# Moving four quotients and a reciprocal around the output projections of an attention and MLP kernel

## The chip, the cores and the metric

The kernel runs on one core of one Trainium2 chip. The metric is device time in microseconds (us) of the whole program. Three timed runs of the kernel before gave a median of 3466.72 us (3463.46 to 3468.94). One more execution was recorded by the profiler; all times of single instructions below come from that one.

The engines are named as the profile names them: PE multiplies matrices (PEld loads its weights), DVE, ACT and POOL work on vectors, SP issues most of the DMA transfers. Each engine takes its instructions in the order in which the program has them, and an instruction that waits holds back all behind it.

## The reference

Two layers, each of attention and an MLP, on one sequence of 2048 rows of width 512 with 32 heads of width 16, all in float32:

```python
x = x + A(layernorm(x), wqkv, wo)
x = x + B(layernorm(x), w1, b1, w2)
# and both once more with the same weights

A: p = softmax(q @ k.T * 16**-0.5);  return (p @ v) @ wo
B: h = x @ w1 + b1;  return (h * tanh(softplus(h))) @ w2        # F = 1792
```

## The kernel before

Every large product is done as three products of rounded parts: each operand is split in a high part and a low part (what is left after rounding), and high*high, high*low and low*high are summed in one PSUM bank. So an output projection tile is 12 matmuls of 128x512: 4 slices of the contraction times 3.

The rows stand in four chunks of 512 (0 to 3). Attention runs over groups of four heads and over chunks; a chunk's sum over keys (softmax not yet divided) is written to DRAM as `raw`, its softmax denominators as `rawsum`. The chunks of the last group end one after the other, and each must then be divided before it can be projected with `wo`. That is what `heads` does for a chunk, as a generator in three kinds of steps:

- first step (`behind(c)`): load the denominators into `sums`, and `raw` into the buffer `ol`.
- second step (`invert(c)`): the reciprocal of `sums` on DVE (line 576); store it to a DRAM scratch `inv` (line 578); load it back, spread over the 16 rows of each head, by eight transfers of 128 KB into the buffer `oh` (line 581). All of these transfers are issued by SP.
- then four steps (`divide(c)`), one for each slice k of the contraction: the quotient `on` = `ol` * `oh` (on DVE for even k, line 590; on POOL for odd k, line 588), its high part cast into `oh` (line 591) and the low part into `ol` (line 592), both on DVE. Each quotient needs all eight transfers.

`project(c)` then does the four tiles t of a chunk: 12 matmuls into a bank of PSUM, then one DVE add of the bank to the residual `x2` (line 607). There are two such banks (tag "n"), so the matmuls of tile t+2 wait for the add of tile t. After each tile's add a function is called that puts other work at this place: `stats` in chunk 0, `middle` in chunk 1, `late` in chunk 2. They advance `norm_steps` (the layer norm of chunk 0 for the MLP: four statistics steps, then steps that scale a tile into `xnm`, transpose it on PE into `tpm`, and split it into `thm` and `tlm`), and they advance the division of the chunks 2 and 3. Chunks 0 and 1 are divided while attention still runs.

The order around the change is written out by hand: `Order` ties each instruction of an engine to the one recorded before it, for the PE, DVE and some ACT instructions of this part. Everything else (the statistics of the later chunks, the MLP's first matmuls `h`, the DMAs) is set between them by a scheduler that goes by the place in the program. SP's transfers all go to one hardware queue, in the order of the code: `load_w1` brings parts 2 to 6 of the first MLP weight (1 MB each; parts 0 and 1 are loaded earlier), `load_w2` those of the second.

Of the kernel before, what the change touches and what calls it, by code (L numbers as in the profile page):

```python
# [51 lines left out]
def kernel(ctx: ExitStack, tc: tile.TileContext, x, wqkv, wo, w1, b1, w2, out):  # L52
# [21 lines left out]
    def b8(shape, dt, name):  # L74
        return blk.tile(shape, dt, tag="blk", name=name)
# [3 lines left out]
    def pbank(tag, name):  # L79
        return ps.tile([P, 512], F32, tag=tag, name=name, bufs=PS_BUFS[tag])  # L80
# [63 lines left out]
    def fetch(kind, j, name):  # L144
        _, a, b = view(kind, j)
        t = b8([P, 2, a, b], F32R, name)
        nc.sync.dma_start(t.bitcast(F32), wparts[kind, j])
        return t
# [12 lines left out]
    def mm3(acc, pairs, first=True, last=True, pe=lambda ins: ins):  # L161
        n = len(pairs)
        for i, (ah, al, bh, bl) in enumerate(pairs):
            pe(nc.tensor.matmul(acc, ah, bh, start=first and i == 0, stop=False))  # L164
            pe(nc.tensor.matmul(acc, ah, bl, start=False, stop=False))  # L165
            pe(nc.tensor.matmul(acc, al, bh, start=False, stop=last and i == n - 1))  # L166

    def norm_parts(src, nm, got, key, tag, fine=False, o=lambda ins: ins):
# [21 lines left out]
        if fine:  # L190
            stats(0)
            rstd(0, 1)
# [18 lines left out]
    def spread(hooks, at, src, nm, got, key):  # L211
        parts = norm_parts(src, nm, got, key, "acc")
        for c, f in at:
            hooks.setdefault((c, f), []).append(lambda: next(parts, None))
# [244 lines left out]
    def load_qkv(l, wts, which, **kw):  # L459
        for j in which:  # L460
            kind, i = ("qk", j) if j < 4 else ("v", j - 4)
            wts[j] = make(kind, i, hi="act", **kw) if l == 0 else fetch(kind, i, f"{kind}{l}{i}")
# [103 lines left out]
    def heads(att, c, o=free):  # L566
        l = att.l
        w = H * CW // P
        sums = t512("he", f"sums{l}{c}")[:, 0:w]
        nc.sync.dma_start(sums, att.sums[c].rearrange("h (x j) -> (h x) j", j=w))  # L570
        ol = b8([P, KT, CW], F32R, f"ol{l}{c}")
        oh = b8([P, KT, CW], F32R, f"oh{l}{c}")
        x, r = ol.bitcast(F32), oh.bitcast(F32)
        nc.sync.dma_start(x, att.raw[c].rearrange("(k p) q -> p k q", p=P))
        yield
        o(nc.vector.reciprocal(sums, sums))
        inv = dram.tile([H, CW], F32, name=f"inv{l}{c}")
        nc.sync.dma_start(inv.rearrange("h (x j) -> (h x) j", j=w), sums)
        n = P // DH
        for h in range(n):  # L580
            nc.sync.dma_start(
                r[ts(h, DH)], inv[h::n, :].unsqueeze(0).to_broadcast([DH, KT, CW])
            )
        yield (oh, ol)
        for k in range(KT):
            on = t512("f", f"on{l}{c}{k}")
            if k % 2:
                nc.gpsimd.tensor_tensor(on, x[:, k], r[:, k], op=ALU.mult)
            else:
                o(nc.vector.tensor_tensor(on, x[:, k], r[:, k], op=ALU.mult))  # L590
            o(nc.vector.tensor_copy(oh[:, k], on))
            o(nc.vector.tensor_tensor(ol[:, k], on, r[:, k], op=ALU.subtract))
            yield

    def project(l, c, parts, wot, x2, o=free, behind=None):
        oh, ol = parts
        for t in range(NCH):
            acc = pbank("n", f"wo{l}{c}{t}")
            mm3(
                acc,  # L600
                [
                    (oh[:, k, ts(t, P)], ol[:, k, ts(t, P)], wot[k // 2][:, 0, k % 2], wot[k // 2][:, 1, k % 2])
                    for k in range(KT)
                ],
                pe=o,
            )
            o(nc.vector.tensor_tensor(x2[:, t], acc, x2[:, t], op=ALU.add))
            if behind:
                behind(t)
# [195 lines left out]
    for l in range(2):  # L805
        if l == 0:
            order = [(m, 0) for m in (0, 4, 1, 5, 2, 6)] + [(m, 1) for m in (0, 4, 1, 5)] + [(3, 0)]
            order += [(0, 2), (4, 2), (7, 0), (2, 1), (6, 1), (0, 3), (4, 3)]
        else:
            order = [(0, 0), (0, 1), (0, 2), (4, 0), (4, 1), (4, 2)]  # L810
            order += [(1, 0), (5, 0), (1, 1), (5, 1), (1, 2), (0, 3), (4, 3)]
        order += [(m, c) for m in (1, 5) for c in range(NCH) if (m, c) not in order]
        order += [("v", c) for c in range(NCH)]
        order += [(m, c) for m in (2, 6, 3, 7) for c in range(NCH) if (m, c) not in order]
        att = qkv(l, wts, tt, order, before, *((front, vst0) if l == 0 else ()))
        wot, w1t, w2t, x2s, tts = [], [], [], [], {}
        xsrc = x if l == 0 else xs

        def load_res(c):
            x2 = b8([P, NCH, D], F32, f"x2{l}{c}")  # L820
            nc.sync.dma_start(x2, xsrc[ts(c, CW), :].rearrange("(t p) d -> p t d", p=P))
            x2s.append(x2)

        hooks, parts, work = {}, {}, {}

        def behind(c, o=free):
            work[c] = heads(att, c, o)
            next(work[c])

        def invert(c):  # L830
            parts[c] = next(work[c])

        def divide(c):
            next(work[c], None)

        def load_wo(i):
            wot.append(fetch("wo", i, f"wo{l}{i}"))

        def load_w1(i):
            w1t.append(fetch("w1", i, f"w1{l}{i}"))  # L840

        def load_w2(i):
            w2t.append(fetch("w2", i, f"w2{l}{i}"))

        if l == 0:
            todo = [("wo", i) for i in range(2)] + [("w1", i) for i in range(7)] + [("w2", i) for i in range(7)]
            for n, (kind, i) in enumerate(todo):
                hooks[30 + 24 * n] = lambda kind=kind, i=i: make(kind, i)
        for i in range(2):
            hooks[STEPS - GSTEPS + 2 * i + 1] = lambda i=i: load_wo(i)  # L850
            hooks[STEPS - GSTEPS + 2 * i + 5] = lambda i=i: load_res(i)
            hooks[STEPS - 1 + i] = lambda i=i: load_w1(i)
        for c, load, inv, div in ((0, 30, 22, 20), (1, 28, 21, 15), (2, 10, 7, None)):
            hooks[STEPS - load] = lambda c=c: behind(c, att.order)
            hooks[STEPS - inv] = lambda c=c: invert(c)
            for k in range(KT if div else 0):
                hooks[STEPS - div + k] = lambda c=c: divide(c)
        att.run(hooks)
        o = att.order
        behind(3, o)  # L860
        for i in range(2, 4):
            load_res(i)
        first = norm_steps(x2s[0], f"m{l}0", tts, 0, "s", o)

        def stats(t):
            next(first)
            if t >= 2:
                divide(2)
            if t == 3:
                invert(3)  # L870

        project(l, 0, parts[0], wot, x2s[0], o, stats)
        for i in range(2, 7):
            load_w1(i)
        def middle(t):
            next(first)
            if t < 2:
                divide(2)

        project(l, 1, parts[1], wot, x2s[1], o, middle)  # L880
        for i in range(4):
            load_w2(i)
        def late(t):
            if t < 2:
                next(first)
            divide(3)

        project(l, 2, parts[2], wot, x2s[2], o, late)
        project(l, 3, parts[3], wot, x2s[3], o)
        for i in range(4, 7):  # L890
            load_w2(i)
        hooks = {}
        for c in range(NCH - 1):
            spread(hooks, [(c, f) for f in range(5, 10)], x2s[c + 1], f"m{l}{c + 1}", tts, c + 1)
        wts, tt = {}, {}
        if l == 0:
            last = NCH - 1
            for f, js in ((2, (0,)), (4, (2,)), (9, (1,)), (11, (3,)), (12, (4,)), (13, (5,))):
                hooks.setdefault((last, f), []).append(lambda js=js: load_qkv(1, wts, js))
            for c in range(last):  # L900
                spread(hooks, [(last, f) for f in range(1 + 4 * c, 6 + 4 * c)], x2s[c], f"q1{c}", tt, c)
        mlp(l, x2s, w1t, w2t, tts, xs if l == 0 else out, hooks)
        if l == 0:
            before = {}
            steps(before, range(2, 12), norm_steps(x2s[last], f"q1{last}", tts, "q", "n", free))
            before.setdefault(11, []).append(lambda: tt.update({last: tts["q"]}))
# [28 lines left out]
```

## Time and profile before

| | |
|---|---|
| median of 3 runs | 3466.72 us (3463.46 to 3468.94) |
| the profiled execution: its own time | 3467.81 us |
| its span (first to last instruction) | 3466.0 us |
| mean granted clock of PE | 0.997 |
| busy: PE, DVE, ACT, POOL | 99%, 86%, 76%, 8% of the span |

A row of a timeline has the start, the duration, the engine, the line of the kernel, the operation, out<-in, the shapes and the number of merged instructions; the square bracket at its end has the idle time of the engine just before and what ended it. SPq is SP's issuing of transfers: the duration is that of issuing, not of the transfer. A row of a windows table has the stretch, its length, each engine's busy time with its instruction count, the granted clock of PE, the busy share of the DMA engines and what they moved in GB/s.

The output projections of layer 0 lie at about 1376 to 1432 us of the span, those of layer 1 at about 3103 to 3159 us.

### The profile page before, as it was taken

The numbers are of one execution on the slowest core, as the hardware profiler recorded it, in microseconds if no ns is written. First come the engines' busy times: TensorE is split into PE (matmuls) and PEld (weight loads), VectorE is DVE, ScalarE is ACT, GpSimd is POOL, SyncE is SP. The second block draws the span as 40 slices with busy tenths as digits, with TensorE's granted clock in tenths as the row PEclk, the third lists the DMA queues.
The fourth block names the chain that finished last, engine by engine and source line by source line (L and its number), as shares of the span: only waits on it lengthen the run. The fifth ranks groups of instructions, "written<-read, shape, count | busy, mean of one in ns | idle before, by whom it ended". The sixth has DMA issues, their size and how long they took to land.

```text
span 3466.0 us, 71144 instructions
## 1 busy us (share of the span) xinstructions
PE 3443.8 (99%) x29075; PEld 1917.8 (55%) x29075; DVE 2966.5 (86%) x4155; ACT 2620.2 (76%) x4865; POOL 282.1 (8%) x329
## 2 busy tenths in 40 slices
PE   9999999999999999999999999999999999999999
PEld 6644444444444445888876444444444444458887
DVE  5699999999999996665537999999999999966554
ACT  3189899989889888356522888988998999874665
POOL 1000000000000001222200000000000000012222
PEclk9999999999999999999999999999999999999999
DMA  7641312213121114500264202112020221154000
GB/s 253 233 102 35 81 43 74 61 54 81 45 58 50 37 55 109 195 13 13 86 199 156 53 15 46 26 36 43 18 56 15 46 37 25 55 136 167 13 13 25
DMA packets 131864, 247.39 MB, mean 71 GB/s; under 512 B 30929, under 2 KB 72401, under 8 KB 116433
## 3 DMA queue, kind: packets, MB, share of 16 engines
q1 hardware_dynamic: 77680, 169.43, 19.6%
q10 hardware_dynamic: 53856, 73.41, 5.8%
q8 instruction: 229, 3.75, 0.5%
q14 instruction: 99, 0.80, 0.1%
HBM read 149.43 MB, written 92.27 MB: 70 GB/s over the span
## 4 chain that ended last, share of the span: by engine, by line
PE 95%; DMA 2%; DVE 2%; ACT 1%; SPq 0%; issue 0%; DVEq 0%; ACTq 0%
PE pv L402 32%; PE sp L355 25%; PE pm L275 8%; PE pn L275 4%; PE h L165 3%; PE h L166 3%; PE h L164 3%; PE mo L164 3%; PE mo L165 3%; PE mo L166 3%; PE qk L164 1%; PE qk L165 1%; PE qk L166 1%; PE va L164 1%; PE va L166 1%; PE va L165 1%
## 5 line engine op out<-in xcount | busy, mean ns | idle before, releaser
L357 ACT ACTIVATE p<-sp 128x512 f32<-128x512 f32 x4040 | 2108.7, 599 | 240.9 <-PE pn L275 145.6
L308 DVE TENSOR_REDUCE mxv<-pn 128x1 f32<-128x512 f32 x2048 | 1306.2, 677 | 6.2 <-PE pn L275 4.4
L293 DVE TENSOR_REDUCE mxv<-pm 128x2 f32<-128x1024 f32 x1024 | 1241.8, 1213 | 78.6 <-PE pm L275 78.6
L355 PE MATMUL sp<-qs,ks 50*128 50x512 f32 x4040 | 1265.9, 445 | 0.0
L402 PE MATMUL pv<-p,va 128*32 128x256 f32 x16384 | 1211.7, 388 | 1.1 <-DVE pt L152 1.1
L355 PEld LDWEIGHTS sp<-qs,ks 50*128 50x128 f32 x4040 | 562.8, 184 | 689.2 <-ACT p L357 620.2
L275 PE MATMUL pn<-ks,qs 48*128 48x512 f32 x2048 | 824.8, 450 | 1.2 <-DVE mxv L308 0.9
L402 PEld LDWEIGHTS pv<-p,va 128*32 128x32 f32 x16384 | 385.0, 108 | 558.1 <-issue 428.4
L275 PE MATMUL pm<-ks,qs 48*128 48x512 f32 x2048 | 437.6, 423 | 1.4 <-DMA ks<-scr 1.4
L275 PEld LDWEIGHTS pn<-ks,qs 48*128 48x128 f32 x2048 | 366.2, 183 | 8.3 <-DVE mxv L308 2.7
L275 PEld LDWEIGHTS pm<-ks,qs 48*128 48x128 f32 x2048 | 193.5, 185 | 64.4 <-issue 7.8
L320 POOL CAST nh<-nm 128x16 fp32r<-128x16 f32 x64 | 12.6, 197 | 2436.7 <-DVE nm L315 2436.7
L666 POOL TENSOR_TENSOR hb<-hb,he 128x512 f32<-128x512 f32 x112 | 148.3, 1324 | 471.9 <-DVE he L663 471.9
L164 PE MATMUL mo<-w,ah 128*128 128x512 f32 x448 | 175.5, 392 | 3.2 <-ACT ah L669 3.0
L166 PE MATMUL h<-thm,w 128*128 128x512 f32 x448 | 175.0, 391 | 0.0
L165 PE MATMUL h<-tlm,w 128*128 128x512 f32 x448 | 174.9, 390 | 0.0
L165 PE MATMUL mo<-w,ah 128*128 128x512 f32 x448 | 174.9, 390 | 0.0
L164 PE MATMUL h<-thm,w 128*128 128x512 f32 x448 | 174.7, 391 | 0.0
L166 PE MATMUL mo<-w,al 128*128 128x512 f32 x448 | 166.1, 390 | 0.0
L668 DVE TENSOR_TENSOR hb<-hb,hr 128x512 f32<-128x512 f32 x112 | 77.3, 690 | 98.9 <-ACT hr L665 73.2
L151 ACT ACTIVATE pt<-qk 128x512 fp32r<-128x512 f32 x64 | 37.9, 598 | 147.7 <-PE qk L166 122.1
L660 ACT ACTIVATE hb<-h,b1t 128x512 f32<-128x512 f32 x112 | 76.9, 686 | 95.4 <-PE h L166 54.1
(133 smaller groups left out, 2590.2 us busy)
## 6 DMA issues: line engine op xcount, KB each, us to landing
scr<-pt ACTq DMA_DIRECT2D x64, 512.0 KB
ks<-scr SPq DMA_DIRECT2D x168, 128.0 KB
qs<-scr SPq DMA_DIRECT2D x168, 128.0 KB
vscr<-vst ACTq DMA_DIRECT2D x32, 512.0 KB
va<-vscr SPq DMA_DIRECT2D x16, 1024.0 KB
w<-w1p SPq DMA_DIRECT2D x14, 1024.0 KB
w<-w2p SPq DMA_DIRECT2D x14, 1024.0 KB
raw<-ot SPq DMA_DIRECT2D x256, 32.0 KB
```

What stands on the lines that cost most here:

```text
L164: pe(nc.tensor.matmul(acc, ah, bh, start=first and i == 0, stop=False))
L165: pe(nc.tensor.matmul(acc, ah, bl, start=False, stop=False))
L166: pe(nc.tensor.matmul(acc, al, bh, start=False, stop=last and i == n - 1))
L275: nc.tensor.matmul(out, qs[h // 2][rows, q0 : q0 + P], ks[h // 2][rows, ts(c, 512)], start=True, stop=True)
L293: self.order(nc.vector.tensor_reduce(self.mxs[b][:, 0:2, qt, c], pm, axis=AX.X, op=ALU.max))
L308: self.order(nc.vector.tensor_reduce(self.mxs[b][:, h, qt, c : c + 1], pm, axis=AX.X, op=ALU.max))
L355: nc.tensor.matmul(sp, ks[h // 2][rows, ts(kt, P)], qs[h // 2][rows, ts(qb, CW)], start=True, stop=True)
L357: return lambda: self.order(nc.scalar.activation(self.pts[s][:, h], sp, AF.Exp, scale=SCALE))
L402: nc.tensor.matmul(acc[ts(h, VW), cols], va[:, kt, h, :], self.pts[s][:, h, cols], start=kt == 0 and half == 0, stop=kt == NKT - 1, skip_g ...
L660: nc.scalar.activation(hb, acc, AF.Identity, bias=b1t[:, f : f + 1])
L666: nc.gpsimd.tensor_tensor(hb, hb, e, op=ALU.mult)
L668: nc.vector.tensor_tensor(hb, hb, r, op=ALU.mult)
```

## The change

Three edits, the same in both layers since the code is shared:

1. The first two `divide(2)` steps (slices 0 and 1 of chunk 2) stand ahead of `project` of chunk 0; before, they stood behind its tiles 2 and 3.
2. The last two `divide(2)` steps (slices 2 and 3) stand behind tiles 1 and 2 of chunk 0; before, behind tiles 0 and 1 of chunk 1.
3. `invert(3)`, chunk 3's reciprocal with its nine transfers, stands in `middle`, behind tile 0 of chunk 1 and the first scaling of the norm; before, it stood behind tile 3 of chunk 0.

```diff
         def stats(t):
             next(first)
-            if t >= 2:
+            if t in (1, 2):
                 divide(2)
-            if t == 3:
-                invert(3)
-
+
+        divide(2)
+        divide(2)
         project(l, 0, parts[0], wot, x2s[0], o, stats)
         for i in range(2, 7):
             load_w1(i)
         def middle(t):
             next(first)
-            if t < 2:
-                divide(2)
+            if t == 0:
+                invert(3)
 
         project(l, 1, parts[1], wot, x2s[1], o, middle)
```

No instruction is added or taken away. SP's queue at this place in layer 0, before (in the names, the digits behind `inv`, `oh`, `x2` and `w1` are the layer and the chunk or part; `w102` is part 2 of the first MLP weight, `w200` part 0 of the second):

```order
L821 DMA x203_18334<-in_A_x_dram 128x4x512
L578 DMA inv03_18421<-sums03_18327 128x128
L581 DMA oh03_18330<-inv03_18421 16x4x512 x8
L147 DMA w102_18431<-w1p2_5723 128x2048
L147 DMA w103_18433<-w1p3_6526 128x2048
L147 DMA w104_18435<-w1p4_7334 128x2048
L147 DMA w105_18437<-w1p5_8118 128x2048
L147 DMA w106_18439<-w1p6_8938 128x2048
L147 DMA w200_18535<-w2p0_9729 128x2048
```

and of the change:

```order
L821 DMA x203_18334<-in_A_x_dram 128x4x512
L147 DMA w102_18428<-w1p2_5723 128x2048
L147 DMA w103_18430<-w1p3_6526 128x2048
L147 DMA w104_18432<-w1p4_7334 128x2048
L147 DMA w105_18434<-w1p5_8118 128x2048
L147 DMA w106_18436<-w1p6_8938 128x2048
L578 DMA inv03_18457<-sums03_18327 128x128
L581 DMA oh03_18330<-inv03_18457 16x4x512 x8
L147 DMA w200_18535<-w2p0_9729 128x2048
```

The store and the eight loads of chunk 3's reciprocal now stand behind the five weight loads of `load_w1`, which follow `project` of chunk 0 in the code.

DVE at the head of the projections, of the change (`on02` are chunk 2's quotients, `x200<-wo000` is the add of chunk 0's tile 0):

```order
L576 RECIPROCAL sums02_18126<-sums02_18126 128x128
L590 TENSOR_TENSOR on020_18336<-ol02_18128,oh02_18129 128x512
L591 CAST oh02_18129<-on020_18336 128x512
L592 TENSOR_TENSOR ol02_18128<-on020_18336,oh02_18129 128x512
L591 CAST oh02_18129<-on021_18340 128x512
L592 TENSOR_TENSOR ol02_18128<-on021_18340,oh02_18129 128x512
L607 TENSOR_TENSOR x200_16592<-wo000_18344,x200_16592 128x512
```

Before, the add of tile 0 followed the reciprocal directly; now five instructions of chunk 2's division stand between them.

DVE where chunk 3's first quotient stands, behind the add of chunk 2's tile 0, of the change:

```order
L179 BN_STATS stm01_18892<-x201_16656 128x6
L179 BN_STATS stm02_19512<-x202_18332 128x6
L590 TENSOR_TENSOR on030_18564<-ol03_18329,oh03_18330 128x512
L180 BN_AGGR mvm01_18893<-stm01_18892 128x2
L180 BN_AGGR mvm02_19513<-stm02_19512 128x2
L591 CAST oh03_18330<-on030_18564 128x512
L175 TENSOR_SCALAR vem01_18894<-mvm01_18893 128x4
L592 TENSOR_TENSOR ol03_18329<-on030_18564,oh03_18330 128x512
L607 TENSOR_TENSOR x202_18332<-wo021_18568,x202_18332 128x512
```

Here the quotient has kept its place ahead of the add of tile 1 (`x202<-wo021`); one BN_STATS that stood between the two before now stands ahead of the quotient.

## The prediction

> **What bounds the kernel now.** I read the head of the page first, then its chain of waits, then PE's waits and the timelines of SP, DVE and PE in the output projections.
>
> ```profile
> span 3466.0 us, 71144 instructions
> PE 3443.8 (99%) x29075; PEld 1917.8 (55%) x29075; DVE 2966.5 (86%) x4155; ACT 2620.2 (76%) x4865; POOL 282.1 (8%) x329
> PE 95%; DMA 2%; DVE 2%; ACT 1%; SPq 0%; issue 0%; DVEq 0%; ACTq 0%
> ```
>
> PE is busy 99% of the span and carries 95% of the chain. So an edit that only moves work of other engines can win no more than PE waits at that place, and it loses whatever new wait it puts into PE. PE's waits between 1370 and 1470 us, which hold layer 0's projections, are one row:
>
> ```profile
> PE tpm L640 <- DVE xnm L630: 1.1, 2, 0.6
> ```
>
> All there is to win is 1.1 us a layer, 2.3 us in both: the first two transposes wait for DVE's scalings, because DVE is full behind chunk 0. What can be lost is read from the queues. SP's timeline, layer 0 and then layer 1:
>
> ```profile
> 1385.59 0.38 SPq L574 DMA_DIRECT2D ol<-raw  x1
> 1386.07 1.01 SPq L821 DMA_DIRECT2D x<-in_A_x_dram  x2
> 1392.54 0.34 SPq L578 DMA_DIRECT2D inv<-sums  x1
> 1396.56 3.62 SPq L581 DMA_DIRECT2D oh<-inv  x8
> 1400.28 3.94 SPq L147 DMA_DIRECT2D w<-w1p  x5
> ...
> 3118.78 0.34 SPq L578 DMA_DIRECT2D inv<-sums  x1
> 3123.55 3.62 SPq L581 DMA_DIRECT2D oh<-inv  x8
> ```
>
> Three loads of 1 MB are issued from 1385.59 on. The 64 KB store of chunk 3's reciprocal is issued at 1392.54, and the loads that read it back only at 1396.56. SP's waits from 1390 to 1412 us have the reason, and chunk 2's rows show the same pair with nothing ahead:
>
> ```profile
> SPq L581 <- DMA inv<-sums: 3.7, 1, 3.7
> ...
> 1366.28 0.34 SPq L578 DMA_DIRECT2D inv<-sums  x1
> 1367.92 4.84 SPq L581 DMA_DIRECT2D oh<-inv  x8
> ```
>
> With an empty queue, the store took 1.6 us from issue to the first read (1367.92 - 1366.28). Behind the three loads it took 4.0 us. The transfers of this queue are served in the order of issue: that is the row on which the forecast rests. DVE and PE at the place where chunk 3's first quotient is taken, in layer 0 and layer 1:
>
> ```profile
> 1406.68 0.69 DVE L590 TENSOR_TENSOR on<-ol,oh 128x512 f32<-128x512 f32 x1 [1.18 <-DMA oh<-inv]
> 1407.38 0.66 DVE L179 BATCH_NORM_STATS2 stm<-x 128x6 f32<-128x512 f32 x1
> 1407.96 0.85 DVE L591 CAST oh<-on 128x512 fp32r<-128x512 f32 x1
> 1409.47 0.68 DVE L607 TENSOR_TENSOR x<-wo,x 128x512 f32<-128x512 f32 x1
> ...
> 3133.39 0.69 DVE L590 TENSOR_TENSOR on<-ol,oh 128x512 f32<-128x512 f32 x1 [1.66 <-DMA oh<-inv]
> ...
> 1409.94 0.62 PE L164 MATMUL h<-thm,w 128*128 128x512 f32 x2
> 1410.40 0.39 PE L164 MATMUL wo<-wo,oh 128*128 128x512 f32 x1
> ...
> 3136.91 0.50 PE L164 MATMUL wo<-wo,oh 128*128 128x512 f32 x1
> ```
>
> DVE already waits there for the eight loads, 1.18 and 1.66 us. Behind the quotient stands the add of chunk 2's tile 1 (1409.47), and PE needs the bank that this add frees to begin tile 3 (1410.40). Now PE comes just as the add is done. Whatever later moment the loads land at goes to PE in full.
>
> **Part 1, the reciprocal behind the weight loads.** On SP, the store and its eight loads are moved past five loads of the first MLP weight. These five wait for no more than buffers of the attention's last steps, which end before 1376.38 (the first projection matmul, quoted below), and so are issued straight behind the two `x` loads, at about 1387 to 1390 us, long before the reciprocal is ready. Their price in the queue:
>
> ```profile
> w<-w1p SPq DMA_DIRECT2D x14, 1024.0 KB
> ...
> 1408.00:1420.00 12.00, 12.00 (x55) 9.93 (x54) 11.27 (x25) 1.32 (x2) 4.38 (x4) 1.00 1.01 423
> 3134.00:3148.00 14.00, 13.88 (x62) 11.15 (x61) 12.10 (x27) 2.38 (x4) 6.14 (x5) 1.00 1.01 427
> ```
>
> In the first windows row nothing but such weight loads run, at 423 GB/s; in layer 1 they run at 427. Five of 1,048,576 bytes take 12.4 and 12.3 us. The store now lands that much later: the eight loads are issued at 1396.56 + 12.4 = 1409.0 and 3123.55 + 12.3 = 3135.9. The reciprocal's own delay on DVE, some 2 us to about 1394.5, lies inside this and costs nothing; without that cover it would be 2 us. From the issue of the eight loads to the quotient it was 1406.68 - 1396.56 = 10.1 us and 3133.39 - 3123.55 = 9.8 us, and DVE was waiting, so this is the loads' own time. The quotient starts at 1419.1 and 3145.7.
>
> From the quotient's start to the end of the add it was 1409.47 + 0.68 - 1406.68 = 3.47 us. One BN_STATS between them is gone from there (0.58 us from its start to the cast's), which leaves 2.9; with 0.1 for PE to start, tile 3 begins 3.0 us behind the quotient: 1422.1 and 3148.7, in place of 1410.40 and 3136.91. **The stall is 11.7 us in layer 0 and 11.8 us in layer 1, together 23.5 us.** In that time PE can do nothing else: its order keeps the two `h` matmuls ahead of tile 3 and all others behind it.
>
> What is late next: the low part of the norm, the other quotients and chunk 3's tiles follow on DVE in their old distances, and PE comes to them about as far behind as before, so I add nothing. The weight loads of the second MLP matrix were behind all of these transfers and still are: the bytes ahead of them are the same, so nothing is late there, and the first one is first used at the MLP's second product, later by the same stall.
>
> The bounds of the landing: the eight loads ran at 140 GB/s here and at 207 in chunk 2's case, where they stood queued behind a load.
>
> ```profile
> 1376.00:1378.00 2.00, 2.00 (x13) 1.38 (x8) 0.00 (x0) 0.60 (x1) 0.00 (x0) 1.00 1.10 207
> 1378.00:1380.00 2.00, 2.00 (x11) 1.65 (x10) 0.58 (x1) 0.00 (x0) 0.00 (x0) 1.00 1.01 418
> 1397.00:1406.00 9.00, 8.47 (x43) 7.07 (x44) 7.98 (x16) 1.80 (x3) 0.19 (x1) 1.00 1.00 140
> ```
>
> At 207 they would take 5.1 us in place of 7.5: 2.4 us less a layer, so the stalls' sum lies between 18.7 and, with 1 us a layer for a store that waits for the slowest of the DMA engines, 25.5. I take 23.5, since the loads will again stand first in an empty stretch, as at 1397.
>
> **Part 2, PE's clock behind the stall.** The trace has two stretches at half clock, in rows of the windows view:
>
> ```profile
> 173.00:176.00 3.00, 2.40 (x8) 0.99 (x8) 3.00 (x6) 2.12 (x4) 0.00 (x0) 1.00 0.32 83
> 176.00:179.00 3.00, 3.00 (x10) 1.56 (x11) 1.36 (x3) 1.11 (x3) 0.00 (x0) 0.56 0.92 320
> 179.00:182.00 3.00, 3.00 (x8) 1.96 (x9) 1.15 (x2) 0.86 (x2) 0.00 (x0) 0.50 0.32 100
> 182.00:185.00 3.00, 2.44 (x22) 0.81 (x19) 2.58 (x4) 2.08 (x5) 0.00 (x0) 0.80 0.36 139
> ...
> 1900.00:1903.00 3.00, 3.00 (x10) 1.66 (x9) 1.50 (x3) 1.57 (x3) 0.00 (x0) 0.52 0.68 169
> 1912.00:1915.00 3.00, 3.00 (x30) 1.11 (x30) 2.08 (x4) 1.43 (x4) 0.00 (x0) 0.71 0.00 0
> ```
>
> PE was idle for 0.6 us of three, and then the clock was granted at 0.56, 0.50 and 0.80: what was lost is 3 x (0.44 + 0.50 + 0.20) = 3.4 us. From 1900 to 1915 a second one lasted about twice as long, 6.8 us lost. A stall of 11.7 us is far longer than these gaps, so I expect a drop in each layer. How much of it falls behind the stall the trace can't show; the bounds are 0 (it ends with the stall) and 6.8. I take 3.0, a little under the shorter stretch: **6 us** in both layers. At half clock PE also comes later to what DVE makes, so nothing is added behind it.
>
> The Trainium skill, "TensorE: Matmul & The Clock Gate", section on the clock gate, says that PE falls to half clock after an idle window of about 3.4 us and comes back after about 3.4 us of work. By that rule the stall is followed by 3.4 to 6.8 us at half clock, an estimate of 1.7 to 3.4 us a layer, and the sum would be 27 to 30 us. The two stretches quoted agree on the half clock; that they came with less than a microsecond of idle time, and one lasted about 13 us, goes beyond it.
>
> **Part 3, the quotients of chunk 2.** They are moved from where DVE is full to where it idles:
>
> ```profile
> 1365.30 0.94 DVE L576 RECIPROCAL sums<-sums 128x128 f32<-128x128 f32 x1
> 1379.42 0.69 DVE L607 TENSOR_TENSOR x<-wo,x 128x512 f32<-128x512 f32 x1 [13.17 <-PE wo L166]
> ...
> 1376.38 0.50 PE L164 MATMUL wo<-wo,oh 128*128 128x512 f32 x1
> 1381.94 0.39 PE L164 MATMUL wo<-wo,oh 128*128 128x512 f32 x1
> ...
> 1357.66 0.69 DVE L590 TENSOR_TENSOR on<-ol,oh 128x512 f32<-128x512 f32 x1 [2.52 <-DMA raw<-ot]
> 1361.48 0.69 DVE L590 TENSOR_TENSOR on<-ol,oh 128x512 f32<-128x512 f32 x1
> ```
>
> DVE idles 13.17 us before its first add, but chunk 2's eight loads are in flight for most of it: the rate jumps from 207 to 418 GB/s, from their small pieces to the weight load behind them, at about 1378.5. Two slices took 1361.48 - 1357.66 = 3.8 us with POOL's quotient beside them, so the first add moves from 1379.42 to about 1382.4 and ends at 1383.1. Tile 2 needs that bank and started at 1381.94: PE waits 1.2 us. Against it stand the two transposes' 1.1 us, since DVE has two slices fewer behind chunk 0. Net 0.1 us a layer, between -1.1 (the loads land earlier) and 1.5; and all of it vanishes in the stall of part 1, which is set by the queue and not by PE.
>
> **The sum.** The profiled execution took 3467.81 us, 1.8 more than its span. With 23.5 + 6 = 29.5 it becomes 3497.3. Its time was 1.1 above the median of 3466.72, so I forecast 3466.72 + 29.5 = **3496 us**.
>
> **The rivals.** *The clock comes back with PE* (15%): the same stall without loss behind it, 3466.7 + 23.5 = 3490. For it: half clock during idle time costs nothing. Against it: both stretches quoted went on under a busy PE.
>
> *A long drop as at 1900* (5%): 6.8 us a layer, 3466.7 + 23.5 + 13.6 = 3504.
>
> *The reciprocal is not held up* (8%), the case on the other side: the queue lets the 64 KB store pass, or the weight loads are issued later than I read. Then the eight loads land within about a microsecond of their old time, PE hardly stalls at tile 3, and the change takes up to 1.1 us a layer from the transposes: 3464 to 3467. It decides as soon as the store lands by 1397. For it: the loads' buffers could be tied to work that I don't see in the trace. Against it: the store's 4.0 us behind three loads.
>
> *The quotients hold DVE up* (3%): chunk 2's loads land later than 1378.5, the adds of chunk 0 are late and tiles 2 and 3 wait. Priced with the store not held up, 1.5 us a layer: 3470. Against it: the rates quoted.
>
> **How the numbers follow.** My forecast has 69%, the others 15, 5, 8 and 3. A measurement of this kernel can tell 0.2% (6.9 us) from no change. The first three cases are slower by more than that: 0.89. The last two lie within 0.2%, so 0.10 for the same. Faster by more isn't to be had, as 2.3 us is all that PE waits there: 0.01 is left for what I overlook. For the range I take the stall's lower bound 18.7 with 1 us a layer of clock loss, and at the upper end the stall's 25.5 with the long drop, 13.6: 3466.7 + 18.7 + 2 = 3487, rounded down to 3486, and 3506. It leaves out the two small cases and some of the rest, 2 in 10 at most.
>
> **What would show it.** In the profile after: SP's row of the five weight loads stands ahead of `inv<-sums`; `oh<-inv` is issued near 1409 and 3136; DVE's quotient `on<-ol,oh` behind it shows about 13 us of idle time ended by `DMA oh<-inv`; PE idles some 12 us ahead of a `wo` matmul, released by DVE's add, twice in the program; then the clock shows about 0.5 for a few us. The transposes' two waits are gone, and a wait of about 1.2 us stands at tile 2 of chunk 0. I am wrong if `oh<-inv` is issued before 1400, or if PE finds other work in the stall.

## The result: 31 us lost, in one stall per layer

The kernel after the change took 3494.48 us (median of 5 runs, 3493.11 to 3498.62), the kernel before 3463.58 us (median of 5, 3462.02 to 3468.94). The ratio is 1.0082 (95% interval 1.0071 to 1.0094; the two medians alone give 1.0089, inside it): slower by 30.9 us, median against median. The profiled execution of the changed kernel took 3498.62 us.

The head of its page and the chain of waits:

```profile
span 3496.8 us, 71131 instructions
PE 3448.6 (99%) x29075; PEld 1922.7 (55%) x29075; DVE 2968.2 (85%) x4155; ACT 2619.9 (75%) x4865; POOL 284.2 (8%) x329
PE 94%; DMA 3%; DVE 1%; ACT 1%; SPq 1%; issue 0%; ACTq 0%; DVEq 0%
```

The work is the same. In the chain PE gave up one per cent, and DMA rose from 2% to 3%: transfers now take more of the path. PE's waits in the projections of layer 0, then of layer 1 (us in total, times, longest):

```profile
PE wo L164 <- DVE x L607: 14.3, 2, 13.0
...
PE wo L164 <- DVE x L607: 12.5, 2, 10.8
```

The 1.1 us a layer at the transposes (`tpm`) are gone, and in their place PE waits twice for DVE's adds: briefly at tile 2 of chunk 0, and long at tile 3 of chunk 2 (13.0 and 10.8 us). SP's timeline, layer 0 and then layer 1, and below it SP's waits from 1385 to 1425 us:

```profile
1386.01 1.01 SPq L821 DMA_DIRECT2D x<-in_A_x_dram  x2
1387.07 3.48 SPq L147 DMA_DIRECT2D w<-w1p  x5
1394.71 0.32 SPq L578 DMA_DIRECT2D inv<-sums  x1
1410.03 3.62 SPq L581 DMA_DIRECT2D oh<-inv  x8
...
3129.22 2.63 SPq L147 DMA_DIRECT2D w<-w1p  x5
3137.86 0.32 SPq L578 DMA_DIRECT2D inv<-sums  x1
3151.61 3.61 SPq L581 DMA_DIRECT2D oh<-inv  x8
...
SPq L581 <- DMA inv<-sums: 14.9, 1, 14.9
```

The five weight loads stand ahead of the store, as was foreseen. The store of 64 KB now takes 15.3 us from its issue to the first read behind it (1410.03 - 1394.71), where it took 4.0. DVE and PE at the end of this wait, and the clock in two stretches of layer 0 and one of layer 1:

```profile
1420.30 0.69 DVE L590 TENSOR_TENSOR on<-ol,oh 128x512 f32<-128x512 f32 x1 [13.41 <-DMA oh<-inv]
...
1421.07 1.33 DVE L591 CAST oh<-on 128x512 fp32r<-128x512 f32 x1
...
1423.04 0.68 DVE L607 TENSOR_TENSOR x<-wo,x 128x512 f32<-128x512 f32 x1
...
1383.52 0.50 PE L164 MATMUL wo<-wo,oh 128*128 128x512 f32 x1 [1.25 <-DVE x L607]
...
1423.78 0.79 PE L164 MATMUL wo<-wo,oh 128*128 128x512 f32 x1 [13.03 <-DVE x L607]
...
1416.00:1423.70 7.70, 0.00 (x0) 0.00 (x0) 3.40 (x8) 0.00 (x0) 2.93 (x2) 0.50 1.04 299
...
1423.70:1429.70 6.00, 5.92 (x14) 4.67 (x15) 6.00 (x13) 0.00 (x0) 1.58 (x2) 0.50 0.45 188
...
3165.20:3170.50 5.30, 5.22 (x12) 4.13 (x13) 5.30 (x12) 0.00 (x0) 1.58 (x2) 0.50 0.53 223
```

DVE idles 13.41 us for the loads, PE 13.03 us for the add that stands behind them in DVE's order, and then PE works 5.9 us (layer 1: 5.2 us) at half clock before the full one is granted. Where the 30.8 us between the two spans came in, by the starts of the same matmuls in both traces:

| stretch | layer 0 | layer 1 |
|---|---|---|
| first projection to tile 3 of chunk 2 | +13.2 us | +12.8 us |
| from there to the MLP's second product | +2.9 us | +2.4 us |
| everything else | -0.6 us | 0.0 us |

In layer 1 the long wait itself is shorter than the stretch grew, because PE comes to it later: its wait at tile 2 is 1.8 us there, and behind that wait the trace has 3.4 us at half clock (from 3126.1 us on, with PE busy), some 1.7 us lost. The end of the stall is set by the queue in both layers.

### The profile page after: what moved, and what is told of

The parts are those of the page before. It is cut to its first block, busy times and chain, and to the rows that moved or that the text cites. A ratio compares the mean times of both kernels' runs of the same rounds, so it can differ in the third digit from the quotient of the medians.

```text
span 3496.8 us, 71131 instructions
## 1 busy us (share of the span) xinstructions
PE 3448.6 (99%) x29075; PEld 1922.7 (55%) x29075; DVE 2968.2 (85%) x4155; ACT 2619.9 (75%) x4865; POOL 284.2 (8%) x329
## 4 chain that ended last, share of the span: by engine, by line
PE 94%; DMA 3%; DVE 1%; ACT 1%; SPq 1%; issue 0%; ACTq 0%; DVEq 0%
PE pv L402 31%; PE sp L355 25%; PE pm L275 8%; PE pn L275 4%; PE h L165 3%; PE h L166 3%; PE h L164 3%; PE mo L164 3%; PE mo L165 3%; PE mo L166 3%; PE qk L164 1%; PE qk L165 1%; PE qk L166 1%; PE va L164 1%; DMA oh<-inv 1%; PE va L166 1%
```

## The experiments

Each diff stands against the changed kernel unless it says otherwise. The ratio is always to the kernel before, run on the same chip beside it. Two theories are tested first. *The order on SP*: the reciprocal's store waits behind the weight loads. *The rival*: the reciprocal itself, which the change makes about 2 us later, or the moved quotients, do the damage.

### Each edit alone

The quotients alone, with the reciprocal back in its old place:

```diff
         def stats(t):
             next(first)
             if t in (1, 2):
                 divide(2)
+            if t == 3:
+                invert(3)
 ...
         def middle(t):
             next(first)
-            if t == 0:
-                invert(3)
```

> Chunk 2's quotients moved as in the change, the reciprocal left behind tile 3 of chunk 0, ahead of the weight loads. My theory (the time comes from the store's place in SP's queue): no stall at tile 3 of chunk 2; about 1.2 us of wait at tile 2 of chunk 0 in each layer, and about 1 us less at the transposes: 3462 to 3466 us, no change that can be measured. Rival (the quotients ahead of the projections hold DVE and so PE up): a good part of the 31 us, 3475 or more.

Measured: 3464.02 us, ratio 0.9999 (0.9991 to 1.0008). The reciprocal alone, against the kernel before:

```diff
         def stats(t):
-            if t == 3:
-                invert(3)
 ...
         def middle(t):
             next(first)
+            if t == 0:
+                invert(3)
             if t < 2:
                 divide(2)
```

> Only the reciprocal moved, the quotients where they were before. My theory: the stall as in the change, 12 to 13.5 us ahead of tile 3 of chunk 2 in each layer and 2 to 3 us of half clock behind it: 3490 to 3497 us. Rival (quotients): near the time of before, under 3475.

Measured: 3495.44 us, ratio 1.0098 (1.0084 to 1.0112). PE's waits in layer 0, first of the quotients alone, then of the reciprocal alone:

```profile
PE wo L164 <- DVE x L607: 2.0, 1, 2.0
...
PE wo L164 <- DVE x L607: 13.8, 1, 13.8
PE tpm L640 <- DVE xnm L630: 1.3, 1, 1.3
```

So the whole loss belongs to the third edit. The first two trade the waits at the transposes, 1.1 us in the kernel before, for one of 1.3 to 2.0 us at tile 2, with no effect on the time that this measurement can tell from nothing. In the trace of the quotients alone they are not quite free: in layer 0 the wait of 2.0 us is followed by 3.4 us at half clock (from 1383.1 us on), and from the first projection to the MLP's second product it takes 57.7 us there against 55.3 before; in layer 1, where the wait is 1.3 us and the clock stays full, it is 55.5 against 55.8.

### The place in the queue, or the lateness

The weight loads are put behind the loads of the reciprocal, and everything else of the change stays:

```diff
         project(l, 0, parts[0], wot, x2s[0], o, stats)
-        for i in range(2, 7):
-            load_w1(i)
 ...
         project(l, 1, ...)
+        for i in range(2, 7):
+            load_w1(i)
```

> The whole change, but the five weight loads called behind the projection of chunk 1 in place of chunk 0, so that SP has the store and its eight loads ahead of them again. My theory: the eight loads are issued near 1397 as before, no stall at tile 3; 3462 to 3467 us. Rival (the reciprocal itself, 2 us later on DVE, is what makes chunk 3 late): a stall of 2 us or more in each layer stays, 3468 or more.

Measured: 3464.02 us, ratio 1.0002 (0.9993 to 1.0011). SP's timeline and PE's waits in layer 0:

```profile
1394.76 0.34 SPq L578 DMA_DIRECT2D inv<-sums  x1
1396.32 3.62 SPq L581 DMA_DIRECT2D oh<-inv  x8
1400.04 3.72 SPq L147 DMA_DIRECT2D w<-w1p  x5
...
PE wo L164 <- DVE x L607: 1.1, 1, 1.1
```

The reciprocal is as late here as in the change (issue at 1394.76 against 1394.71), yet its loads follow 1.6 us behind and no long wait is left. Lateness is not the cause; what stands ahead in the queue is. The dose, with two of the five loads ahead and three behind:

```diff
-        for i in range(2, 7):
+        for i in range(2, 4):
             load_w1(i)
 ...
         project(l, 1, ...)
+        for i in range(4, 7):
+            load_w1(i)
```

> The whole change, but only two of the five weight loads ahead of the store, three behind the projection of chunk 1. My theory (2.45 us of queue for each load of 1 MB): the eight loads issued about 4.9 us later than before, near 1401.5; a stall of about 5 us in each layer, 3473 us, and up to 5 us more if the clock drops behind so short a stall. Rival (a fixed cost of crossing any such load, or of the buffers): 3490 or more, or 3465 or less.

Measured: 3477.61 us, ratio 1.0045 (1.0032 to 1.0057). SP's timeline and PE's waits, layer 0 and layer 1:

```profile
1385.50 1.01 SPq L821 DMA_DIRECT2D x<-in_A_x_dram  x2
1386.56 1.37 SPq L147 DMA_DIRECT2D w<-w1p  x2
1395.18 0.32 SPq L578 DMA_DIRECT2D inv<-sums  x1
1401.06 3.61 SPq L581 DMA_DIRECT2D oh<-inv  x8
...
PE wo L164 <- DVE x L607: 5.1, 2, 2.7
...
PE wo L164 <- DVE x L607: 6.1, 2, 4.8
```

From the issue of the two `x` loads to that of the reciprocal's eight it is 15.6 us with two loads ahead, and 24.0 us with five (1410.03 - 1386.01). From two to five that is 2.8 us for each load of 1 MB, a little more than the 2.5 us that its bytes take at 423 GB/s. From the first projection to tile 3 of chunk 2 it takes 5.6 and 4.8 us longer than before in the two layers, where about 5 was expected. From there to the MLP's second product it takes another 1.7 and 2.1 us longer: even these waits of 2.7 and 4.8 us bring stretches of 3.4 and 6.8 us at half clock (from 1414.5 and 3138.3 us on).

### The add behind the quotient

How the late loads reach PE is the next link. Here the loads stay as late as in the change, but chunk 3's four quotients stand behind the last add of chunk 2, so that no add waits behind a quotient:

```diff
         def late(t):
 ...
-            divide(3)
+            if t == 3:
+                for _ in range(KT):
+                    divide(3)
```

> The whole change, but chunk 3's four quotients all behind the last add of chunk 2, so that no add of chunk 2 stands behind a waiting quotient on DVE. The loads land as late as in the change (near 1420), but PE goes on with tile 3 and some 30 matmuls of the MLP, 9.5 us of work. My theory (the stall reaches PE through the add behind the quotient): the stall shrinks from 13 to 3 to 5 us a layer, 3471 to 3480 us. Rival (PE needs the quotients themselves at once): the stall stays above 10 us, 3488 or more.

Measured: 3471.11 us, ratio 1.0018 (1.0009 to 1.0026). SP's row and PE's waits in layer 0:

```profile
1408.87 3.61 SPq L581 DMA_DIRECT2D oh<-inv  x8
...
PE wo L164 <- DVE x L607: 2.5, 1, 2.5
PE wo L164 <- DVE oh L591: 1.9, 2, 1.6
PE wo L166 <- DVE ol L592: 0.9, 1, 0.9
```

The loads are issued at 1408.87, nearly as late as in the change, and most of the stall is gone: chunk 2's tile 3 runs beneath them. So two things together make the stall: the queue makes the loads late, and DVE's order lets the adds of a chunk that is ready wait behind a quotient that is not. What is left in layer 0 is the wait at tile 2 of chunk 0, 2.5 us, and chunk 3's own wait for its parts, 1.9 + 0.9 = 2.8 us.

### The clock behind the stall

PE is given 54 spare matmuls, whose sums nothing uses, ahead of tile 3 of chunk 2. They keep PE busy for 12.4 us where it stood still, and the queue is untouched:

```diff
+            if t == NCH - 1 and idle:
+                spare = pbank("acc", ...)
+                for n in range(idle):
+                    o(nc.tensor.matmul(spare, oh[:, 0, 0:P], wot[0][:, 0, 0], ...))
 ...
-        project(l, 2, ..., late)
+        project(l, 2, ..., late, 54)
```

> The whole change with 54 spare matmuls (12.2 us) into an unused bank ahead of tile 3 of chunk 2, where PE stands still; their sums are not used. My theory (half clock behind the stall is a term of its own, 2 to 2.5 us a layer): the clock stays full there, and from tile 3's start to the MLP's first second-matrix product it is about 21.5 us as before the change, in place of 24; the time 3489 to 3493 us, less than the change's by 2 to 5. Rival (what follows the stall is lost to DVE being late, not to the clock): those 24 us stay, the time is that of the change or 1 more.

Measured: 3491.22 us, ratio 1.0073 (1.0060 to 1.0085). PE's timeline and the clock behind the spare matmuls, layer 0:

```profile
1415.85 12.40 PE L601 MATMUL spare<-wo,oh 128*128 128x512 f32 x54
1428.09 0.39 PE L164 MATMUL wo<-wo,oh 128*128 128x512 f32 x1
...
1428.00:1434.00 6.00, 6.00 (x26) 4.36 (x25) 6.00 (x13) 0.00 (x0) 1.29 (x1) 1.00 0.66 247
```

With PE kept busy the full clock is granted on, and from tile 3 to the MLP's second product it takes 22.3 and 23.1 us in the two layers, against 24.2 and 23.9 in the change and 21.3 and 21.5 before. In neither layer is there a half-clock stretch at this place any more. Some 0.45 us of the rest is the two `h` matmuls, which the scheduler put behind the spare ones here, and in layer 1 another 0.6 us is a wait for chunk 3's first part. The time gains less than these stretches, because in layer 0 the spare matmuls run on: DVE's add has freed the bank at 1427.24, and tile 3 starts at 1428.09. The two intervals of the times overlap, so it is the trace and not the time that shows this term. The loads are as late as in the change and only PE's idle time is gone: it is the idle time, not the late data, that brings the half clock.

### Another queue for one side

If one queue's order is the cause, a second queue should help. First the five weight loads go through ScalarE's queue:

```diff
 ...
         for i in range(2, 7):
-            load_w1(i)
+            load_w1(i, eng=nc.scalar)
```

> The whole change, but the five weight loads issued by ACT, which has a hardware queue of its own; they start at the same time. If it is the order within SP's queue that holds the store up, it passes them: the store follows the x loads, which now share the DMA engines with the weights, near 1402, the eight loads land near 1414, the stall is about 7 us a layer: 3475 to 3485 us. If it is the bytes in flight whatever the queue, the stall stays at 13 us: 3492 or more.

Measured: 3494.49 us, ratio 1.0081 (1.0069 to 1.0094): the expectation missed, and nothing was won. SP's timeline, SP's waits, and what the two queues moved from 1390 to 1398 us (q10 is ScalarE's, q1 is SP's; packets, MB, share of 16 engines):

```profile
1385.08 0.38 SPq L574 DMA_DIRECT2D ol<-raw  x1
...
1401.87 0.34 SPq L578 DMA_DIRECT2D inv<-sums  x1
1408.77 3.62 SPq L581 DMA_DIRECT2D oh<-inv  x8
...
SPq L578 <- DMA ol<-raw: 14.9, 1, 14.9
...
q10 hardware_dynamic: 352, 2.62, 78.0%
q1 hardware_dynamic: 353, 0.72, 23.4%
```

The two queues took turns by packets, 352 to 353, and ScalarE's packets are about 3.6 times as large. The Trainium skill, "DMA: Bandwidth & Descriptors", section "Queues, rings and completion order", says that each engine goes round the queues that have work, a packet at a time; these two counts agree. So SP's `raw` and `x` transfers, which went ahead of the weights before, got a fifth of the bytes (0.72 of 3.34 MB). And the store was not even issued until 1401.87: SP waited for the landing of `ol<-raw`, eight transfers earlier if the transfers of both queues are counted, although the store does not need its data.

That points to a second link between the queues, so the store and the eight loads of chunk 3 go through ScalarE's queue in the last experiment, and the weight loads stay on SP's:

```diff
-        nc.sync.dma_start(inv..., sums)
+        eng.dma_start(inv..., sums)
 ...
-            nc.sync.dma_start(
+            eng.dma_start(
 ...
-        behind(3, o)
+        behind(3, o, eng=nc.scalar)
```

> The change, with the store of the fourth chunk's reciprocal and its eight loads issued by ScalarE's queue; the five weight loads stay on SyncE's. If the place in one queue's row of transfers is all that holds the reciprocal up, the store lands within some 3 us, the loads follow at once, no stall of PE over 3 us is left ahead of tile 3 of chunk 2, and the time is 3464 to 3470 us. If a transfer also waits for the landing of the one eight issues before it, whichever queue that is in, the store gets by, but the later of its eight loads wait for the weight loads' landings as before (oh<-inv is complete only at about 1414 to 1418 us of the span, PE stalls 9 to 14 us in each layer), ScalarE is held behind these issues, and the time is 3488 to 3505 us.

Measured: 3501.07 us, ratio 1.0115 (1.0098 to 1.0132), the second case. ScalarE's issues, its wait from 1380 to 1430 us, and PE's waits in layer 0:

```profile
1397.27 0.33 ACTq L578 DMA_DIRECT2D inv<-sums  x1
1404.30 11.21 ACTq L581 DMA_DIRECT2D oh<-inv  x8
...
ACT thm L643 <- DMA oh<-inv: 37.6, 1, 37.6
...
PE tpm L640 <- DVE xnm L630: 10.5, 1, 10.5
PE wo L164 <- DVE x L607: 2.9, 2, 2.1
```

The store does get by: 7.0 us from issue to the first read, with five weight loads in flight, against 15.3 in one queue. But issuing the eight loads takes 11.21 us where SP needed 3.62. By the landings recorded in the trace, the sixth is issued at 1408.61, as the fourth weight load has landed (1408.59), and the seventh at 1414.71, as the fifth has (1414.69): each is the transfer eight issues earlier. Meanwhile ScalarE can't copy `thm` (its idle time before that copy, 37.6 us, ends with these issues), DVE waits 13.0 us for the copy, and PE's transposes wait behind DVE. The trace's record of each transfer names the semaphore that its landing raises: in both of these kernels SP's and ScalarE's transfers take the same eight in turn. The sixth load has that of the fourth weight load, the seventh that of the fifth, and in the kernel before this one the store has that of `ol<-raw`. So both queues draw on one set of eight landing marks, and a second queue is not an independent path in this program.

### A version that takes both gains

Chunk 2's quotients spread out (behind tiles 0, 1 and 2 of chunk 0 and tile 1 of chunk 1), and the weight loads behind the reciprocal's:

```diff
         def stats(t):
-            if t in (1, 2):
+            if t < 3:
                 divide(2)
-        divide(2)
-        divide(2)
 ...
         def middle(t):
             next(first)
             if t == 0:
                 invert(3)
+            if t == 1:
+                divide(2)
```

(The weight loads as in the third experiment.)

> A version that may beat both: the quotients of chunk 2 behind tiles 0, 1 and 2 of chunk 0 and tile 1 of chunk 1, the reciprocal as in the change, the five loads behind the projection of chunk 1. By the rows, the two waits at the transposes and the wait at tile 2 of chunk 0 are all gone or below 0.4 us, the loads of chunk 3's reciprocal as before: 1 to 2 us less than before, 3460 to 3464 us. Rival: a new wait at tile 1 of chunk 1 takes it back, 3463 to 3467.

Measured: 3464.28 us, ratio 0.9998 (0.9989 to 1.0007). This is 0.3 us above the expected range and inside the rival's, but no wait stands at tile 1 of chunk 1, so the rival's reason is not what is seen. PE's waits in the projections are the least of all kernels, and both lie at tile 3 of chunk 2, layer 0 and then layer 1:

```profile
PE wo L164 <- DVE x L607: 0.6, 1, 0.6
...
PE wo L164 <- DVE x L607: 0.8, 1, 0.8
```

The gain in the traces is 0.6 us in both layers together (first to last projection matmul: 54.7 and 54.9 us against 54.9 and 55.3), which is far below what the time can tell. No kernel of this study beats the kernel before.

## Why the prediction was right

**What bounds the kernel.** Right. All that PE waited for here was 1.1 us a layer, and no kernel that got rid of it was measurably faster.

**Part 1, the stall.** Right in its mechanism, place and both layers, and a little short in size: 13.2 and 12.8 us, together 26.0, against 23.5, and 0.5 us above its own upper bound of 25.5. That bound allowed 1 us a layer for the store, for which no row was given; the loads were issued 1.0 us later than forecast in layer 0, and in layer 1 0.1 us later, counted from the 15.6 us that layer 0 had lost. That a slow DMA engine is the reason is not shown. In layer 0 the eight loads were issued at 1410.03, against 1409.0, and the loads themselves took 10.3 us to the quotient against 10.1. The other half microsecond is the step from the quotient to tile 3, costed at 3.0 us because one BN_STATS leaves it. It took 3.5 us. The cast behind the quotient took 1.33 us in place of 0.85, with POOL's quotient beside it:

```profile
1420.33 1.78 POOL L588 TENSOR_TENSOR on<-ol,oh 128x512 f32<-128x512 f32 x1 [26.94 <-DMA oh<-inv]
...
1406.72 1.80 POOL L588 TENSOR_TENSOR on<-ol,oh 128x512 f32<-128x512 f32 x1 [9.53 <-DMA oh<-inv]
```

(The first row is of after, the second of before.) Without the BN_STATS the cast starts at 1421.07, when POOL has 1.04 us left, against 0.56 us in the kernel before: 0.48 us more, as much as the cast grew. What the removed instruction gave back went into a slower cast. No run removes POOL's quotient by itself, but the traces leave little else: in the projections of all eleven kernels' traces, 123 casts begin beneath a quotient on POOL, and each ends 0.28 or 0.29 us after that quotient does; two more begin in its last 0.05 us and take 0.41 us, which is what a cast takes alone (0.40 to 0.43 us). In layer 1 the quotient started at 3161.81 against 3161.3 (the forecast 3145.7 plus the 15.6 us that layer 0 had already lost), and the same half microsecond came on top. The reason that the store is held by the place in one queue was shown by moving only the weight loads (1.0002), by the dose, and by the store that took 7.0 us in the other queue where it took 15.3 in this one.

**Part 2, the clock.** Right: 3.0 us a layer were taken, 2.9 and 2.4 measured. The half clock lasted 5.9 and 5.2 us beyond the end of the stall, which at half speed is 3.0 and 2.6 us. The Trainium skill, "TensorE: Matmul & The Clock Gate", section on the clock gate, counts activity in windows of about 3.4 us that run on freely. From this, an estimate, the full clock would come back 3.4 to 6.8 us after the work does; both layers lie inside that, and the kernel with PE kept busy shows that it is idle time which brings the half clock.

**Part 3, the quotients.** Right. The wait at tile 2 was 1.25 us in layer 0 (1.2 forecast) and 1.8 in layer 1, the transposes' waits vanished, and alone these edits were worth nothing that the time shows (0.9999). What it leaves out is the clock behind this wait. Of the nine waits at tile 2 between 1.7 and 2.8 us in the traces of all kernels, seven are followed at once by 3.4 us at half clock; of the six of 1.6 us and less, none is.

**The sum and the time.** 29.5 us were forecast and 30.9 measured, the stall being 2.5 us longer and the clock's loss 0.7 less. That the time came out 1.5 us under the forecast of 3496 has another reason: the median of before is 3463.58 over five runs, where the prediction had 3466.72 from three. So the total comes so close by luck in part: the loss was 1.4 us more than forecast, and the time it was added to 3.1 us less.

**The rivals.** *The clock comes back with PE* fell by the two rows at 0.50 under a busy PE. *A long drop* fell because of the 13.7 us at half clock in each layer, more than half lay in the stall, where it costs nothing. *The reciprocal is not held up* (3464 to 3467) is what the kernel with the weight loads behind shows, at 3464.02; its price was right and its condition wasn't met. *The quotients hold DVE up* did occur in a small form, at 1.3 to 2.0 us at tile 2 in the kernel with the quotients alone. What the transposes gave back covered it in layer 1; in layer 0, with the half clock behind it, it did not (2.3 us more than before), and the time, 3464.02, is too coarse to show it.

## What to carry to other kernels

Before moving a small store whose result is read back soon, count the bytes that will then be ahead of it in its queue: here 64 KB behind 5 MB cost 13 us a layer, while the reciprocal itself, 2 us later, cost nothing. Then look at what stands behind the waiting instruction on its engine: most of the loss came only because an add that was ready stood behind a quotient that was not. And when a stall of about 2 us or more reaches PE, allow for the half clock behind it in the sum: 1.7 us behind most of the short ones here, 2.4 to 2.9 behind the long ones.

## What the runs showed of the hardware beyond this

A second queue did not divide the DMA engines evenly by bytes: 352 packets against 353, but 2.62 MB against 0.72. Two engines' queues were also tied together by the order of issue, as the issues held until 1401.87 (a store behind an unrelated load) and 1414.71 show.

Stretches at half clock also come and go elsewhere in the program, where nothing was changed. The windows view of one place in layer 0, of before and of the kernel with the spread quotients:

```profile
176.00:179.00 3.00, 3.00 (x10) 1.56 (x11) 1.36 (x3) 1.11 (x3) 0.00 (x0) 0.56 0.92 320
...
176.00:179.00 3.00, 3.00 (x18) 1.88 (x18) 1.92 (x3) 2.13 (x5) 0.00 (x0) 1.00 0.68 254
```

The profiled execution of the latter had no such stretch before its last microseconds, and a span of 3455.8 us, the shortest seen; its median is that of the kernel before all the same. By the clock's record in the traces, these stretches last 3.4, 6.8, 10.2 or 13.7 us, multiples of one length (the end of the program cuts one off). The spread from run to run goes with them: of the runs of the kernel before on one chip, the fastest took 3458.13 us at a mean clock of 1.000 and the slowest 3469.97 at 0.997. Single profiles that differ by less than this should be compared by stage.
